# Attention and MLP on one core: two query groups share the first keys, half-size score operations at first, tiles turned by DMA, a larger tanh, W1 in halves

## The chip, the cores and the metric

One core of one Trainium2 chip. The metric is the device time of one execution in microseconds (us). Each run of a kernel was timed beside runs of the kernel before on the same chip. The span is the length of the profiled execution; the time is about 2 us more than the span in the same run.

Engines: PE does matrix products, PEld loads their weights, ACT does the exponentials and tanh, DVE and POOL do vector work, SP issues the DMA transfers. A q behind an engine's name in a view (SPq) is its sequencer, which issues.

## The reference

Input is x, 2048 rows of 1024. It is normalised by row, goes through attention of 32 heads of width 32 and, beside it, through a gated MLP of width 3584; all in bf16.

```python
xn = layernorm(x)
q, k, v = heads(xn @ wqkv)                      # 32 heads, width 32
p = softmax(q @ k.T * 32 ** -0.5)
s = heads_back(p @ v) @ wo
h = gelu_tanh(layernorm(xn) @ w1 + b1)
g = silu(h @ w2 + b2)
return x + s * g
```

## The kernel before

The kernel doesn't write instructions in the order in which they run. It makes operations with an assumed duration each; a list scheduler in the program, run once when the kernel is built, then fixes the order on every engine. I call its result the static order.

The assumed durations, and ACT's:

```python
def c_act(n):
    return 49 + 0.836 * n          # ns: 905 for 1024 elements
...
def chunk(item, fn, occ, R, mode="f", W=()):
    o = add("PE", lambda e, fn=fn, item=item: fn(e, item.bank), occ, TL, R, W, item=item, mode=mode)
```

The start. Tiles of 128 rows are normalised (statistics on DVE, the power and the normalising on POOL, the first two on DVE), turned on PE, and copied by ACT. Keys are projected by pairs of tiles:

```python
chunk(it, fn, n * 56, [("xnb", t % 4), ("ident",)])                 # turn a tile on PE
...
act(lambda e: e.activation(dst, src(), ACT.Copy), c_act(128 * n), [], W, 0, it)
...
pro_q += [tr_item(lo), tr_item(lo + 1), k_pair_item(n, False)]
```

A unit is four heads, 256 queries and one pair of key tiles: a score operation of eight matmuls and two exponentials of 128 x 1024. There are 512 units, so 1024 exponentials. Eight units make a group, whose sums over the keys stay in one bank of PSUM, where PE's results land, until it is normalised. Scores go round a ring of six banks; as long as the tiles come in (the first 8 units) four of them serve the scores and two more the projections and sums:

```python
NARROW = 8
k0 = 0 if u < NARROW else 2 * (u - NARROW) + 2
b0 = [(2 * k0 + j) % 6 for j in range(4)]
...
for h in range(2):
    x = act(lambda e, h=h: e.activation(P[pi][:, 2 * h:2 * h + 2].rearrange("p j k q -> p (j k q)"),
                                        ps[:, pr[h] * 1024:(pr[h] + 1) * 1024], ACT.Exp, scale=SCALE),
            c_act(1024), [("S", pr[h])], [("P", pi, h)], 0)
```

The tanh of the MLP is 512 wide. (The last four output items, of eight matmuls each, run after the last exponential.)

```python
act(lambda e: e.activation(ut_t[i3][:], ut_t[i3][:], ACT.Tanh, scale=GC * GA), c_act(512), ...)
```

The softmax here doesn't subtract the row's maximum and nothing guards it: scores larger than these inputs give would overflow.

## Time and profile before

| | before |
|---|---|
| time, median | 1061.66 us (1060.71 to 1061.72, 3 runs) |
| span of the profiled run | 1060.2 us, granted clock 0.998 |
| first exponential starts | 12.69 us |
| ACT's next work after the 32nd exponential starts (a tanh; before it the start, after it the full middle) | 63.45 us |
| last exponential ends | 1046.09 us |
| from there to the end of the span, "the tail" | 14.1 us |
| ACT busy / PE busy / DVE busy | 1028.9 / 1026.5 / 946.9 us |

Three views matter. The chain that ended last says which engine's work fills the span. The waits of an engine add up its idle time by what ended it. The timeline gives one row for a row of like operations: start, length, engine, line, operation, output and input, how many, and in brackets the idle time before and what ended it. I read the kernel as three parts: the start, the middle in which ACT is always busy, and the tail.

### The profile page before, as it was taken

The page shows a single profiled execution, that of the slowest core. Times are in us where ns is not written, and L with a number is a line of the kernel's source. Part 1 is how long each engine was busy: PE and PEld are TensorE (multiplying, and loading weights), DVE is VectorE, ACT ScalarE, POOL GpSimd, SP SyncE. Part 2 cuts the span into 40 slices and gives each one's busy share as a digit, 9 for nine tenths or more (in the row PEclk, how much of TensorE's full clock was granted, in tenths as well). Part 3 has the DMA queues.
Part 4 walks back from the last instruction along what each step waited for, and adds up shares of the span by engine and source line. Part 5 has one row for each costly group of instructions (what it writes and reads, how often), then busy time and mean ns, then how long its engine had stood idle before and what let it go on. Part 6 is the DMA issues. An engine that isn't in the chain of part 4 may idle for free.

```text
span 1060.2 us, 32647 instructions
## 1 busy us (share of the span) xinstructions
PE 1026.5 (97%) x14502; PEld 643.7 (61%) x14562; DVE 946.9 (89%) x1585; ACT 1028.9 (97%) x1186; POOL 31.2 (3%) x42
## 2 busy tenths in 40 slices
PE   7999999999999999999999999999999999999998
PEld 5756466556665566566665566466665666665443
DVE  8479898999999998899989998999999998978996
ACT  4999999999999999999999999999999999999994
POOL 5500000000000000000000000000000000000000
PEclk9999999999999999999999999999999999999999
DMA  9335166522674466423763476224765776662442
GB/s 268 111 96 158 42 179 190 144 76 71 186 207 126 113 193 196 113 57 112 206 192 105 122 199 195 74 76 121 212 180 151 221 217 190 179 197 70 134 140 87
DMA packets 285798, 156.52 MB, mean 148 GB/s; under 512 B 23642, under 2 KB 276570, under 8 KB 285658
## 3 DMA queue, kind: packets, MB, share of 16 engines
q1 hardware_dynamic: 285658, 154.44, 51.0%
q8 instruction: 114, 1.87, 0.8%
q14 instruction: 26, 0.21, 0.1%
HBM read 142.35 MB, written 12.06 MB: 146 GB/s over the span
## 4 chain that ended last, share of the span: by engine, by line
ACT 93%; PE 4%; DVE 2%; DMA 1%; issue 0%; SPq 0%; POOL 0%; POOLq 0%
ACT P L1067 86%; ACT ut L939 5%; PE ps L668 3%; ACT gw L971 2%; DVE stats L823 1%; DMA hT<-in_A_x_dram 1%; PE ps L663 1%; ACT big L814 0%; PE ps L1058 0%; PE ps L803 0%; DVE yT L911 0%; POOL gw L847 0%; DVE V L740 0%; DVE mv L825 0%; SPq L693 0%
## 5 line engine op out<-in xcount | busy, mean ns | idle before, releaser
L1067 ACT ACTIVATE P<-ps 128x1024 bf16<-128x1024 f32 x1024 | 986.8, 1243 | 5.3 <-PE ps L1058 5.3
L1087 DVE TENSOR_TENSOR PA<-P 128x2048 bf16<-128x2048 bf16 x243 | 294.7, 1215 | 25.4 <-ACT P L1067 24.1
L668 PE MATMUL ps<-yT,w1r 128*128 128x256 bf16 x1792 | 234.9, 275 | 2.3 <-DVE xb L931 1.1
L668 PE MATMUL ps<-w2r,hT 128*128 128x256 bf16 x1792 | 226.9, 273 | 0.3 <-DVE nv L1121 0.2
L668 PEld LDWEIGHTS ps<-yT,w1r 128*128 128x128 bf16 x1792 | 162.1, 98 | 60.5 <-issue 28.6
L668 PEld LDWEIGHTS ps<-w2r,hT 128*128 128x128 bf16 x1792 | 162.2, 98 | 51.0 <-issue 30.5
L1091 DVE TENSOR_TENSOR PA<-PA 128x1024 bf16<-128x1024 bf16 x219 | 147.7, 684 | 1.4
L663 PE MATMUL ps<-P,V 128*32 128x256 bf16 x4096 | 142.8, 274 | 0.6 <-DVE xb L931 0.4
L668 PE MATMUL ps<-big,qk 128*128 128x512 bf16 (+2 forms) x522 | 120.9, 357 | 5.7 <-issue 2.1
L668 PE MATMUL ps<-qk,big 128*128 128x256 bf16 (+1 forms) x723 | 121.2, 305 | 2.5 <-issue 1.3
L663 PEld LDWEIGHTS ps<-P,V 128*32 128x32 bf16 x4096 | 97.7, 96 | 33.1 <-issue 19.6
L1058 PE MATMUL ps<-QKT 32*128 32x256 bf16 x2048 | 101.7, 273 | 7.4 <-ACT P L1067 5.9
L1058 PE MATMUL ps<-qk 32*128 32x256 bf16 x2048 | 101.9, 273 | 6.2 <-ACT P L1067 2.1
L939 ACT ACTIVATE ut<-ut 128x512 f32<-128x512 f32 x112 | 94.5, 855 | 0.0
L668 PEld LDWEIGHTS ps<-qk,big 128*128 128x128 bf16 x736 | 65.3, 98 | 41.5 <-issue 13.3
L931 DVE TENSOR_TENSOR xb<-ps,b1T 128x512 bf16<-128x512 f32 x112 | 76.6, 684 | 13.9 <-PE ps L668 12.6
L941 DVE SCALAR_TENSOR_TENSOR hT<-ut,xb 128x512 bf16<-128x512 f32 x112 | 76.4, 684 | 5.9 <-ACT ut L939 5.2
L668 PEld LDWEIGHTS ps<-big,qk 128*128 128x128 bf16 x568 | 47.7, 98 | 52.4 <-issue 15.6
L1058 PEld LDWEIGHTS ps<-QKT 32*128 32x128 bf16 x2048 | 30.3, 92 | 76.6 <-ACT P L1067 75.9
L937 DVE SCALAR_TENSOR_TENSOR ut<-sq,xb 128x512 f32<-128x512 bf16 x112 | 76.1, 682 | 0.3
L1058 PEld LDWEIGHTS ps<-qk 32*128 32x128 bf16 x2048 | 30.4, 92 | 71.6 <-ACT P L1067 67.4
L663 PE MATMUL ps<-PA,ones 128*32 128x256 bf16 x1068 | 56.0, 274 | 0.3 <-DVE PA L1091 0.3
(75 smaller groups left out, 532.2 us busy)
## 6 DMA issues: line engine op xcount, KB each, us to landing
w1r<-in_B_w_dram SPq DMA_DIRECT2D x112, 512.0 KB, 4.4
w2r<-in_B_w_dram SPq DMA_DIRECT2D x128, 448.0 KB, 4.4
qk<-in_A_wqkv_dram SPq DMA_DIRECT2D x16, 256.0 KB, 3.2
g_scratch<-gw SPq DMA_DIRECT2D x32, 128.0 KB, 3.0
o_scratch<-ot SPq DMA_DIRECT2D x56, 64.0 KB, 2.8
big<-o_scratch SPq DMA_DIRECT2D x28, 128.0 KB, 3.5
hT<-in_A_x_dram SPq DMA_DIRECT2D x10, 256.0 KB, 5.5
qk<-in_A_wqkv_dram SPq DMA_DIRECT2D x4, 512.0 KB, 4.4
```

The source lines that it names most:

```text
L663: ins = e.matmul(dst(j), lhsT=lhsT(j), rhs=rhs(j), start=start, stop=stop, tile_position=(0, 32 * j), skip_group_check=True)
L668: return e.matmul(dst, lhsT=lhsT, rhs=rhs, start=start, stop=stop, skip_group_check=True)
L823: dve(lambda e, t=t, c=c: e.bn_stats(stats[:, t, c, :], xst[t][:, c * 512:(c + 1) * 512]), 600, [XS(t)], [("st", t, c)], 1)
L931: dve(lambda e: e.tensor_tensor(xb_t[i3][:].rearrange("p (k t) -> p k t", k=2), bank(it.bank).rearrange("p (k t) -> p k t", k=2), b1T[:, 2 ...
L937: dve(lambda e: e.scalar_tensor_tensor(ut_t[i3][:], sq_t[p % 2][:], 1.0 / GA, xb_t[i3][:], op0=ALU.add, op1=ALU.mult), c_f32(512), [("sq", ...
L939: act(lambda e: e.activation(ut_t[i3][:], ut_t[i3][:], ACT.Tanh, scale=GC * GA), c_act(512), [("ut", i3)], [("ut", i3)], 1)
L941: dve(lambda e: e.scalar_tensor_tensor(hT[:, hs].rearrange("p k t -> p (k t)"), ut_t[i3][:], 1.0, xb_t[i3][:], op0=ALU.add, op1=ALU.mult), ...
L971: act(lambda e: e.activation(zh_t[zi], z_t[zi], ACT.Tanh, scale=0.5), c_act(512), [("z", zi)], [("zh", zi)], 1)
L1058: ins = e.matmul(bank(b0[j], kk * 256, (kk + 1) * 256), lhsT=QKT[sl][32 * j:32 * j + 32, 1, kb * 128:(kb + 1) * 128], rhs=QKT[sl][32 * j:3 ...
L1067: x = act(lambda e, h=h: e.activation(P[pi][:, 2 * h:2 * h + 2].rearrange("p j k q -> p (j k q)"), ps[:, pr[h] * 1024:(pr[h] + 1) * 1024], ...
L1087: pa = dve(lambda e: e.tensor_tensor(PA_all[:, a0:a0 + 2].rearrange("p u j q -> p (u j) q"), P_all[:, p0:p0 + 2, :, 0, :].rearrange("p u j ...
L1091: pb = dve(lambda e: e.tensor_tensor(PA[a0][:], PA[a0][:], PA[a1][:], op=ALU.add), c_b16(1024), [("PA", a1)], [("PA", a0)], PBPRIO)
```

## The change

Its intent: take work off ACT, which carries the chain, and give it exponentials earlier.

1. From the third tile on, a tile is turned by a transposing DMA and not by PE and an ACT copy; tiles 2 and 3 are normalised on DVE.
2. The first two query groups share each pair of keys as it comes, so four exponentials come with each pair, not two.
3. For the first 16 units a score operation covers half a unit; both groups' sums are open in banks 4 and 5.
4. One tanh of 1024 takes the place of two of 512; the DVE operations around it are merged too.
5. The sums of P for the denominator are added over four units.
6. Seven of eight matmuls of the last four output items are summed and put aside early.
7. W1 comes in two halves, PE's pieces are single matmuls, and some constants differ.

The core of the diff, much cut:

```diff
-    NARROW = 8
-    plan.narrow = NARROW
+    NARROW = 16
+    plan.narrow = 2 * NARROW
...
         def c_act(n):
-            return 49 + 0.836 * n
+            return 52.5 + 0.836 * n
+
+        def c_acts(n):
+            return 92 + 0.836 * n
...
-            pro_q += [tr_item(lo), tr_item(lo + 1), k_pair_item(n, False)]
+            for t in (lo, lo + 1):
+                if t < TD:
+                    pro_q.append(tr_item(t))
+                else:
+                    add("SP", lambda e, t=t: e.dma_start_transpose(out=xnT[:, :, t * 128:(t + 1) * 128], in_=xnb[t % 4]),
+                        1290, 0, [("xnb", t % 4)], [("xnT", t, h) for h in range(2)], 0, sem=f"tp{t % 4}", nbytes=262144)
+            pro_q.append(k_pair_item(n, False))
...
-            act(lambda e: e.activation(ut_t[i3][:], ut_t[i3][:], ACT.Tanh, scale=GC * GA), c_act(512),
-                [("ut", i3)], [("ut", i3)], 1)
+            act(lambda e: e.activation(ut_t[i2][:], ut_t[i2][:], ACT.Tanh, scale=GC * GA), c_acts(1024),
+                [("ut", i2, 0), ("ut", i2, 1)], [("ut", i2, 0), ("ut", i2, 1)], 1)
...
-            plan.s_queue.append(o)
+            if u < NARROW:
+
+                for h in range(2):
+                    plan.s_queue.append(add("PE", lambda e, h=h: s_fn(e, (2 * h, 2 * h + 1)), 232.0, TL + 30, R, [("S", pr[h])], mode="r"))
+            else:
+                plan.s_queue.append(add("PE", lambda e: s_fn(e, range(4)), 235.0, TL + 30, R, [("S", pr[0]), ("S", pr[1])], mode="r"))
...
+                    for pos, (i, kp) in enumerate([(0, 0), (0, 1), (1, 0), (1, 1)] + [(i, kp) for kp in range(2, NKP) for i in range(2)]):
+                        x, vc = unit(i * 8 + kp, two[i], pos)
...
+                if qb == PART:
+
+                    for t2 in range(2):
+                        wo_load(NQB - 1, t2)
+                        for nh in range(2):
+                            wo_item(NQB - 1, t2, nh, 0, 7)
```

## The prediction

> **What bounds the kernel now.** I read the page first, then the waits of ACT, the groups of ACT and DVE by shape, and the timeline of the start and of the end. The page:
>
> ```profile
> span 1060.2 us, 32647 instructions
> ...
> PE 1026.5 (97%) x14502; PEld 643.7 (61%) x14562; DVE 946.9 (89%) x1585; ACT 1028.9 (97%) x1186; POOL 31.2 (3%) x42
> ...
> ACT 93%; PE 4%; DVE 2%; DMA 1%; issue 0%; SPq 0%; POOL 0%; POOLq 0%
> ```
>
> PE and ACT both read 97% busy, so the first row decides nothing; the chain that ended last does: 93% of it is ACT. The waits of ACT are three rows over the whole execution:
>
> ```profile
> ACT big L814 <- PE ps L803: 11.2, 7, 6.0
> ACT P L1067 <- PE ps L1058: 5.3, 5, 3.0
> ACT L715 <- PEq L1284: 0.7, 1, 0.7
> ```
>
> The 1024 exponentials waited only 5.3 us. The timeline of ACT shows where (start, length, what, idle before):
>
> ```profile
> 8.19 1.51 ACT L814 ACTIVATE big<-ps 128x1024 bf16<-128x1024 bf16 x2 [5.98 <-PE ps L803]
> 12.69 1.94 ACT L1067 ACTIVATE P<-ps 128x1024 bf16<-128x1024 f32 x2 [2.98 <-PE ps L1058]
> 16.01 1.02 ACT L814 ACTIVATE big<-ps 128x1024 bf16<-128x1024 bf16 x1 [1.38 <-PE ps L803]
> ...
> 22.49 1.95 ACT L1067 ACTIVATE P<-ps 128x1024 bf16<-128x1024 f32 x2
> ...
> 61.63 1.94 ACT L1067 ACTIVATE P<-ps 128x1024 bf16<-128x1024 f32 x2 [0.92 <-PE ps L1058]
> ```
>
> After 62 us ACT never waits again; the stretches 70 to 1043 us of the windows view are 100% ACT. So the span has three parts: a start in which ACT does copies and idles, a saturated middle, and a tail. In the chain, 29 exponentials in a row take 26.56 us, so one costs 0.9165 us of ACT, not the 1.243 us of its mean duration (neighbours overlap). Between 63.45 and 1045.73 us the exponentials and the small tanh fill all time; taking the exponentials out leaves 0.51 us for each 512-wide tanh.
>
> The account closes: first exponential 12.7; 1024 x 0.9165 = 938.5; 144 tanh x 0.51 = 73.4; 14 tile copies after the first exponential x 0.92 = 12.9; idle after the first exponential 1.38+0.15+2.46+0.63+0.21+0.19+0.35+0.50+0.68+0.92 = 7.5; tail from the last exponential's end at about 1045.7 to 1060.2, 14.5. The sum is 1059.5 of 1060.2. The tail is this:
>
> ```profile
> 1046.71 0.43 PEld L663 LDWEIGHTS ps<-P,ones 128*32 128x32 bf16 x16
> ...
> 1047.48 0.45 DVE L1118 STREAM_TRANSPOSE nt<-ps 128x256 f32<-128x256 f32 x1 [1.04 <-PE ps L663]
> ...
> 1049.15 0.41 DVE L1128 TENSOR_TENSOR qk<-ps,nt 128x256 bf16<-128x256 f32 x1
> ...
> 1056.86 0.69 DVE L1221 SCALAR_TENSOR_TENSOR w1r<-ps,w1r 128x512 bf16<-128x512 f32 x1 [0.58 <-PE ps L668]
> 1057.58 0.43 DVE L1228 TENSOR_TENSOR w1r<-w1r 128x512 bf16<-128x512 bf16 x1
> ```
>
> The normalised last group is ready at 1049.56, and the four output items of eight 512-wide matmuls then hold PE until 1056.8.
>
> **What the Trainium skill says.** "ScalarE: Activation LUTs", section What ACT_TABLE_LOAD costs: 0.833 ns per element plus 186 ns with immediates, back-to-back ones overlapping by about 93 ns. That is a fixed 93 ns per ACTIVATE; the trace agrees: 0.51 - 512 x 0.833/1000 = 0.083 us for the tanh and 0.063 us for the exponential. "VectorE: DVE Perf Modes", section The TRN2 errata, says that SBUF-source operations pay a fixed cost per instruction: the trace has 0.416 us for 512 and 0.684 us for 1024 bf16 elements of tensor_tensor, so 0.148 us fixed. "DMA: Bandwidth & Descriptors", section Latency and other measured facts, gives transposing DMAs 261 GB/s with a non-contiguous middle dimension, 350 to 400 otherwise. A tile of 262,144 bytes is then, as an estimate from that page, 0.7 to 1.0 us of transfer; no transposing DMA is in this trace. "TensorEngine Tiling (Array Packing)", Key Properties, says that a change of tiling mode drains TensorE: the trace shows about 0.2 us of idle weight load around each score operation.
>
> **The change part by part.**
>
> *Tile copies.* 14 of 16 tiles are turned by DMA. This takes 14 x 0.92 = 12.9 us off ACT and 14 x about 0.5 = 7 us off PE. They stood in the prologue, where they delayed exponentials, so I count them fully: -12.9 us, provided that exponentials are there to fill their place.
>
> *Two groups per key pair.* That provides them. Now each pair of key tiles releases one unit, 2 exponentials, 1.83 us; with two groups it releases 3.67 us. Supply per pair from the timeline: POOL needs 0.71+0.19+2x1.20 = 3.3 us; DVE 4 x 0.6 + 0.3 for statistics plus an evacuation, about 3.2 us. So 3.3 in against 3.67 out: once going, ACT should not starve. The gap after the first unit stays: ACT is done at about 14.5. Tiles 2 and 3 are now normalised on DVE (0.55 us each), which I place at 12.3 to 13.4; then a DMA issue, 2.5 to 3.5 us to land (plain loads of that size took 3 to 5.5 us, the longer ones in a queue), 0.9 us of projection, an evacuation of 0.4, the score: exponentials at 19 to 20. That is 4.5 to 5.5 us idle. I add 2 to 4 us for stalls in the half-unit stage: the two rings alternate with about 0.2 us semaphore, 0.2 chunk, 0.1 mode change, 0.25 score and 0.25 to ACT against 0.9165 us, which just doesn't fit every time. Idle 8 us instead of 7.5: +0.5 us.
>
> *Larger tanh.* 112 + 32 tanh of 512 become 56 + 16 of 1024: 72 fixed costs of 0.083 us: -6.0 us, directly on the path.
>
> *The tail.* Seven of eight matmuls of the last four output items are done earlier. After 1049.5 remain 4 x 0.22 us on PE, overlapped with 4 evacuations at 0.65, two f32 adds at 0.6 on DVE (two on POOL beside them), and 2.2 us for the store: the end about 5.5 us after the normalisation, against 10.6 now. The partial sums' own work lies under ACT. I take -4.5 us.
>
> *Sums over four units.* A third add on DVE, at most 123 x 0.684 = 84 us, and 28 more second adds (19 us) and 4 first ones (5 us), against 168 merged GELU operations and 16 gate products saving 0.148 us each (27 us): DVE would go from 947 to 1028 us, 99% of the new span. The schedule drops adds that come late, so I expect part of them. PE saves: 1276 ones-matmuls are 319 groups of four at 0.11 us, 35 us; at full use 160 remain, saving 17 us, with half the third adds dropped 11 us. PE isn't the bound, so 0 us, but it keeps PE behind ACT.
>
> *W1 in halves, smaller chunks, other issue constants.* Transfers already come in time; 0 us.
>
> The sum: -12.9 + 0.5 - 6.0 - 4.5 = -22.9 us; 1061.66 - 22.9 = 1038.8. A perfect start (the first gap only) would give about 1035.5. The schedule looks tuned against measured costs, so I lean to the better side: **1037.5 us**.
>
> **Rivals.** (a) *PE becomes the bound in the prologue.* From 19 to 46 us it must do six key projections (5.3), a query pair (0.9), two value items (3.5), 28 half scores at 0.23 plus two mode changes (11.8) and the first products (3.5): 25 of 27 us. Then five value items and twelve delayed products (14 us) meet ten units' scores (4.3) in 18.3 us. For it: PE is 30.1 of 33 us busy there now. Against: value items can wait. It would make 1040 to 1047.
> (b) *The transposing DMAs are slow or queue behind loads.* If a tile took over 1.83 us steadily, 12 tiles would lag: at 2.5 us, 8 us more, 1045 to 1047. Against: the loads beyond tile 7 and W1 are held back.
> (c) *DVE becomes the bound in the middle* and delays evacuations, then scores: merged operations of 1.2 us block it longer. For: 89% now, 96% or more after. Against: its own waits and the dropping of adds. It would make 1042 to 1060.
> (d) *PE in the middle.* Counting 0.11 us per 256-wide matmul, 0.22 per 512, 0.43 per score with changes gives some 1000 us now, 94%. ACT's gain squeezes it by 2%, the ones-matmuls return 1 to 1.7%: about neutral.
>
> **Range and chances.** Copies and tanh, 19 us, are nearly sure as work; what stalls give back is 0 to 10 us in the start and perhaps as much in the middle; the tail is 4 to 5. So 1028 to 1048 at 8 in 10. The line of 2% lies at 1040.4, three microseconds above my figure: faster 0.65, within 0.32, slower 0.03.
>
> **What would show it.** Right: ACT waits after the first exponential of 6 to 10 us, mostly one before 20 us; 32 exponentials done by about 48 us instead of 63; two ACT copies instead of sixteen; tanh of 1024 at 0.94 us; under 11 us after the last exponential; 100% ACT in the middle. Wrong: score waits spread over the middle (c, d), ACT waits of over 12 us before 60 us (a if PE is full there, b if PE waits for DMA), a first exponential later than 13.5 us, or transposes landing in over 4 us.

## The result, and the profile after

The changed kernel took 1057.97 us (median of 4 runs, 1056.18 to 1058.75); the kernel before took 1061.18 us (1060.6 to 1061.72) in the same rounds. Ratios here are the mean time of one kernel's fast runs over that of the other's of the same rounds, so not quite the ratio of the medians: 0.9967, 95% interval 0.995 to 0.9985. That is a real gain of 0.3% and within the 2% that count as the same. Predicted were 1037.5 us, with 1028 to 1048 as the range: 20 us too good. A gain of over 2% had been given 0.65, what came 0.32.

The page of the changed kernel, the rows that answer to those of before:

```profile
span 1055.8 us, 31978 instructions
...
PE 1024.0 (97%) x14230; PEld 632.8 (60%) x14230; DVE 967.9 (92%) x1463; ACT 1010.3 (96%) x1100; POOL 28.6 (3%) x40
...
ACT 88%; PE 7%; DMA 2%; DVE 2%; SPq 0%; POOL 0%; issue 0%; DVEq 0%; POOLq 0%
```

ACT lost 18.6 us of work, as predicted (12.9 of copies, some 6 of tanh), but the span lost only 4.4. ACT's share of the chain fell from 93% to 88%: PE and the DMA took its place. Its waits in the changed kernel (in all, times, longest):

```profile
ACT P L1134 <- PE ps L1120: 23.3, 8, 7.0
ACT big L845 <- PE ps L834: 7.2, 2, 6.4
```

Exponentials waited 23.3 us where it was 5.3. ACT's timeline in the changed kernel shows where:

```profile
15.25 1.94 ACT L1134 ACTIVATE P<-ps 128x1024 bf16<-128x1024 f32 x2 [4.21 <-PE ps L1120]
24.23 7.44 ACT L1134 ACTIVATE P<-ps 128x1024 bf16<-128x1024 f32 x8 [7.05 <-PE ps L1120]
...
44.00 1.94 ACT L1134 ACTIVATE P<-ps 128x1024 bf16<-128x1024 f32 x2 [1.59 <-PE ps L1120]
46.53 1.94 ACT L1134 ACTIVATE P<-ps 128x1024 bf16<-128x1024 f32 x2 [0.60 <-PE ps L1120]
50.68 7.51 ACT L1134 ACTIVATE P<-ps 128x1024 bf16<-128x1024 f32 x8 [2.21 <-PE ps L1120]
64.61 12.94 ACT L1134 ACTIVATE P<-ps 128x1024 bf16<-128x1024 f32 x14 [6.43 <-PE ps L1120]
```

All of it is in the start. The 32nd exponential ends at 58.19 us instead of 63.57, but the gap of 6.43 us behind it more than takes that back: ACT's next work, which was to come 12.4 us sooner, starts at 64.61 instead of 63.45 us. (Before, that is a tanh, and the 33rd exponential starts at 63.97; now it is the 33rd exponential.) From there on ACT is full, as before. The table by part:

| part | before | after | difference | predicted |
|---|---|---|---|---|
| start, to ACT's next work after 32 exponentials | 63.45 | 64.61 | +1.2 | -12.4 |
| middle, to the end of the last exponential | 982.6 | 977.0 | -5.6 | -6.0 |
| tail | 14.1 | 14.15 | 0 | -4.5 |
| span | 1060.2 | 1055.8 | -4.4 | -22.9 |

So 13.6 us are missing in the start, 4.5 in the tail, 0.4 in the middle. Four places show why.

**The second pair of keys.** PE's timeline of the changed kernel:

```profile
9.97 0.86 PE L834 MATMUL ps<-ident,gw 128*128 128x128 bf16 x8 [1.35 <-DVE gw L867]
10.62 3.38 PE L701 MATMUL ps<-big,qk 128*128 128x128 bf16 x32
...
19.04 1.05 PE L701 MATMUL ps<-qk,big 128*128 128x256 bf16 x8 [2.73 <-DMA big<-gw]
20.33 3.52 PE L701 MATMUL ps<-big,qk 128*128 128x256 bf16 x16 [0.23 <-DMA big<-yT]
23.78 0.42 PE L1120 MATMUL ps<-qk 32*128 32x256 bf16 x8
```

The 32 matmuls at 10.62 take 3.38 us; before they took 1.96. The granted clock between 10 and 14 us is 0.55 to 0.60 of full speed, after PE stood idle 0.98 and 1.35 us. The same comes back at 20.33: sixteen matmuls in 3.52 us after an idle stretch of 2.73, which ended when the transposed tile had come.

**The transposing DMA.** SP's issues in the changed kernel (start, time taken by the issue):

```profile
15.69 1.35 SPq L894 DMA_TRANSPOSE big<-gw  x1
17.09 1.29 SPq L894 DMA_TRANSPOSE big<-yT  x1
...
38.33 0.51 SPq L940 DMA_DIRECT2D w2r<-in_B_w_dram  x1
38.88 3.98 SPq L894 DMA_TRANSPOSE big<-gw  x2
42.90 0.58 SPq L933 DMA_DIRECT2D w1r<-in_B_w_dram  x1
43.52 1.24 SPq L894 DMA_TRANSPOSE big<-gw  x1
```

One issue takes 1.24 to 2 us of SP, in one row with the weight loads. Issued at 15.69, the tile is used at 19.04: 3.35 us. The DMA view of the first 60 us gives the median from issue to landing:

```profile
big<-gw SPq DMA_TRANSPOSE x10, 4.3
big<-yT SPq DMA_TRANSPOSE x4, 4.4
```

POOL normalises pairs at 19.29, 23.83, 27.99, 31.40, 35.78 and 39.40 us, one in about 4.0 us, not one in 3.3 as I had taken. The last pair's DMA is issued at 43.5 and 44.8 us, its keys are projected at 48.7.

**The change of ring.** From 48.7 us on no tile is missing, and yet ACT idles 6.43 us before 64.61. The windows view of the changed kernel (stretch, its length, busy PE, PEld, DVE, ACT, POOL, then clock, DMA share, GB/s):

```profile
48.70:63.70 15.00, 14.97 (x203) 9.60 (x199) 4.54 (x10) 7.51 (x8) 0.00 (x0) 1.00 0.84 203
```

PE is busy 14.97 of 15.00 us while ACT is busy half the time. The 17th unit is the first with whole score operations and needs banks 4 and 5. These hold the sums of the two groups that share keys, so all their products must be done first, and so all values of all tiles projected first. The chain over this stretch is PE throughout: value projections, products of P and V, the last two at 61.5; then DVE moves the sums out and makes the query tile, and the score starts at 64.17.

**The tail.** The end of PE's timeline in the changed kernel:

```profile
1042.46 1.69 PE L701 MATMUL ps<-qk,big 128*128 128x512 bf16 x7
1043.98 0.38 PE L701 MATMUL ps<-qk 128*128 128x512 bf16 x1
...
1045.92 1.67 PE L701 MATMUL ps<-qk,big 128*128 128x512 bf16 x7
1047.43 1.24 PE L701 MATMUL ps<-qk 128*128 128x512 bf16 x5
```

And of DVE's:

```profile
1043.92 0.42 DVE L1224 TENSOR_TENSOR qk<-ps,nt 128x256 bf16<-128x256 f32 x1
...
1048.46 2.48 DVE L1281 SCALAR_TENSOR_TENSOR w1r<-ps,w1r 128x512 bf16<-128x512 f32 x4
...
1051.70 1.28 DVE L1286 TENSOR_TENSOR w1r<-w1r,hT 128x512 bf16<-128x512 bf16 x2
```

The last group is normalised at 1044.34 us, but the four matmuls that wait for it come last on PE, at 1047.7, some 3.3 us later. Ahead of them PE does three whole output items of another group, 24 matmuls of 0.216 us, 5.2 us from 1042.5 on. Seven eighths of the last items had indeed been put aside; other work of PE had been put off into the tail in their place. What follows the four matmuls takes another 8.1 us, where the prediction had 5.5 for all that follows the normalisation: on DVE the other group's last evacuation and add (0.69 and 0.84 us in the chain) come in among the four evacuations (2.39), and the stores end 2.8 us after the last add.

### The profile page after: what moved, and what is told of

It is laid out like the page before. It is cut to its first block, busy times and chain, and to the rows that moved or that the text cites. A ratio compares the mean times of both kernels' runs of the same rounds, so it can differ in the third digit from the quotient of the medians.

```text
span 1055.8 us, 31978 instructions
## 1 busy us (share of the span) xinstructions
PE 1024.0 (97%) x14230; PEld 632.8 (60%) x14230; DVE 967.9 (92%) x1463; ACT 1010.3 (96%) x1100; POOL 28.6 (3%) x40
## 4 chain that ended last, share of the span: by engine, by line
ACT 88%; PE 7%; DMA 2%; DVE 2%; SPq 0%; POOL 0%; issue 0%; DVEq 0%; POOLq 0%
ACT P L1134 82%; ACT ut L995 5%; PE ps L701 5%; ACT gw L1031 1%; PE ps L696 1%; PE ps L1120 1%; DMA big<-yT 1%; DMA hT<-in_A_x_dram 1%; DVE ut L854 0%; DMA big<-gw 0%; DVE w1r L1281 0%; DVE V L771 0%; SPq L715 0%; POOL gw L886 0%; SPq L723 0%
## 5 line engine op out<-in xcount | busy, mean ns | idle before, releaser
L1134 ACT ACTIVATE P<-ps 128x1024 bf16<-128x1024 f32 x1024 | 965.3, 1245 | 23.4 <-PE ps L1120 23.3
L1164 DVE TENSOR_TENSOR PA<-P 128x2048 bf16<-128x2048 bf16 x246 | 298.7, 1216 | 15.8 <-ACT P L1134 15.1
L1169 DVE TENSOR_TENSOR PA<-PA 128x1024 bf16<-128x1024 bf16 x204 | 138.2, 681 | 1.5
L701 PE MATMUL ps<-big,qk 128*128 128x512 bf16 (+2 forms) x568 | 134.6, 368 | 1.5 <-DMA big<-gw 0.8
L701 PE MATMUL ps<-qk,big 128*128 128x256 bf16 (+1 forms) x736 | 127.3, 306 | 3.2 <-DMA big<-gw 2.7
L1120 PE MATMUL ps<-qk 32*128 32x256 bf16 x2048 | 106.0, 273 | 8.6 <-ACT P L1134 7.6
L701 PEld LDWEIGHTS ps<-qk,big 128*128 128x128 bf16 x736 | 64.9, 98 | 45.0 <-issue 17.7
L995 ACT ACTIVATE ut<-ut 128x1024 f32<-128x1024 f32 x56 | 72.5, 1295 | 0.0
L998 DVE SCALAR_TENSOR_TENSOR hT<-ut,xb 128x1024 bf16<-128x1024 f32 x56 | 67.9, 1212 | 1.3 <-ACT ut L995 1.0
L993 DVE SCALAR_TENSOR_TENSOR ut<-hT,xb 128x1024 f32<-128x1024 bf16 x56 | 68.0, 1214 | 0.0
L696 PE MATMUL ps<-PA,ones 128*32 128x256 bf16 x896 | 46.4, 275 | 0.0
```

Source lines behind the costliest of these rows:

```text
L696: ins = e.matmul(dst(j), lhsT=lhsT(j), rhs=rhs(j), start=start, stop=stop, tile_position=(0, 32 * j), skip_group_check=True)
L701: return e.matmul(dst, lhsT=lhsT, rhs=rhs, start=start, stop=stop, skip_group_check=True)
L993: dve(lambda e, r=r: e.scalar_tensor_tensor(ut_t[i2][:, r], h[:, r], 1.0 / GA, xb[:, r], op0=ALU.add, op1=ALU.mult), c_f32(r.stop - r.star ...
L995: act(lambda e: e.activation(ut_t[i2][:], ut_t[i2][:], ACT.Tanh, scale=GC * GA), c_acts(1024), [("ut", i2, 0), ("ut", i2, 1)], [("ut", i2, ...
L998: dve(lambda e, r=r: e.scalar_tensor_tensor(h[:, r], ut_t[i2][:, r], 1.0, xb[:, r], op0=ALU.add, op1=ALU.mult), c_f32(r.stop - r.start), [ ...
L1120: ins = e.matmul(bank(b0[j], kk * 256, (kk + 1) * 256), lhsT=QKT[sl][32 * j:32 * j + 32, 1, kb * 128:(kb + 1) * 128], rhs=QKT[sl][32 * j:3 ...
```

## The experiments

All kernels gave the right result, but for e5 to e7, which leave out products on purpose (the check doesn't notice them). Each was run five rounds (e5 to e7 three) beside the kernel before, four to six runs of each. What I read from each profile:

| kernel | time, median (range), us | ratio to before, 95% | first exp. | waits after it | last exp. ends | tail |
|---|---|---|---|---|---|---|
| before | 1061.18 (1060.6-1061.72) | | 12.69 | 2.3 | 1046.09 | 14.1 |
| after | 1057.97 (1056.18-1058.75) | 0.9967 (0.995-0.9985) | 15.25 | 19.1 | 1041.65 | 14.15 |
| e1 | 1065.03 (1062.92-1066.44) | 1.0036 (1.0023-1.0049) | 15.96 | 19.3 | 1049.28 | 14.1 |
| e2 | 1057.64 (1056.46-1058.94) | 0.9969 (0.9957-0.9982) | 15.04 | 11.6 | 1034.14 | 21.5 |
| e3 | 1060.67 (1060.37-1062.34) | 1.0003 (0.9991-1.0016) | 13.98 | 11.2 | 1044.93 | 13.8 |
| e4 | 1064.45 (1063.31-1066.46) | 1.003 (1.0017-1.0044) | 14.98 | 27.4 | 1050.25 | 14.15 |
| e5 | 1067.19 (1065.5-1067.75) | 1.0054 (1.0039-1.0069) | 12.36 | 7.0 | 1051.22 | 14.7 |
| e6 | 1064.73 (1062.71-1067.21) | 1.0041 (1.0022-1.006) | 14.82 | 23.8 | 1046.51 | 14.2 |
| e7 | 1054.57 (1053.69-1054.87) | 0.9936 (0.9921-0.9951) | 15.10 | 13.9 | 1037.51 | 14.1 |
| e8 | 1049.1 (1048.72-1050.11) | 0.9887 (0.9873-0.9902) | 13.99 | 11.2 | 1034.09 | 12.6 |
| e9 | 1065.11 (1063.23-1065.85) | 1.0035 (1.0022-1.0048) | 14.90 | 26.1 | 1049.54 | 14.2 |
| e10 | 1054.83 (1052.55-1055.71) | 0.9939 (0.9927-0.9951) | 14.95 | 12.8 | 1035.22 | 18.4 |
| e11 | 1057.04 (1054.85-1061.21) | 0.997 (0.9956-0.9984) | 14.74 | 8.0 | 1044.28 | 12.2 |
| e12 | 1052.27 (1050.6-1054.71) | 0.9924 (0.9912-0.9936) | 13.65 | 10.0 | 1036.10 | 12.2 |
| e13 | 1064.01 (1062.02-1067.61) | 1.0029 (1.0014-1.0043) | 12.55 | 2.0 | 1046.93 | 14.5 |
| e14 | 1062.13 (1060.57-1065.39) | 1.0012 (0.9999-1.0025) | 15.12 | 25.4 | 1049.66 | 12.6 |
| e15 | 1063.51 (1061.77-1064.04) | 1.0015 (1.0003-1.0027) | 14.81 | 23.0 | 1047.09 | 12.6 |
| e16 | 1058.44 (1054.7-1063.39) | 0.9977 (0.9958-0.9997) | 13.66 | 20.8 | 1041.65 | 14.15 |
| e17 | 1050.49 (1049.31-1052.16) | 0.9903 (0.9889-0.9917) | 13.45 | 13.9 | 1036.19 | 12.6 |
| e18 | 1049.56 (1048.23-1050.89) | 0.9888 (0.9872-0.9905) | 14.31 | 12.4 | 1035.61 | 12.6 |

The waits after the first exponential are those of exponentials for scores or products; copies' own waits are not in them. Where I subtract two experiments' times, their rounds may differ; the kernel before had medians of 1060.7 to 1061.7 in all of them. Parts 3, 5, 6 and 7 of the change were not undone by themselves; part 3 was extended (e2), and of part 6 only the order at the end was tried (e10, e15).

The theory at the outset: the change removes what the prediction said, but the start is not set by ACT any more. It is set by when keys come and by the change of ring, and the tail by what PE has left. The rival: the removed work itself was worth little, since PE bounds the whole kernel.

### One part undone: the tanh

```diff
-            act(... ut_t[i2][:] ..., ACT.Tanh ...), c_acts(1024), ...
+            for j in range(2):
+                act(... ut_t[i2][:, j * 512:(j + 1) * 512] ..., ACT.Tanh ...), c_acts(512), ...
```

(and the same for the gate's tanh)

> The changed kernel with each 1024-wide tanh of ACT issued again as two of 512; all else as changed. Theory 1 (ACT sets the pace from 65 us on, so its fixed costs count one for one): 72 more fixed costs of 0.078 to 0.083 us, 5.6 to 6.0 us slower than the changed kernel, 1063.5 to 1064 us. Rival (PE or DVE sets the pace in the middle and the merge was hidden): within 1 us of the changed kernel's 1058.0. ACT idle before 65 us as in the changed kernel, 19 us after the first exponential, in both.

The two-step tanh costs 7.1 us of time, against 72 x 0.083 = 6.0 worked out. The last exponential ends 7.6 us later, 1.2 of them waits of exponentials after 100 us. The merge is worth what the prediction said or a little more, so ACT does bound the middle; the time is 1 us above what theory 1 expected.

### The change of ring

```diff
+    NWIDE = 24
...
+            if n in (4, 5):
+                pro_q.append(q_pair_item(n - 2))
...
-            k0 = 0 if u < NARROW else 2 * (u - NARROW) + 2
+            k0 = 0 if u < NWIDE else 2 * (u - NWIDE) + 2
...
-            if u < NARROW:
+            if u < NWIDE:                     # half-unit scores for eight units more
```

> The changed kernel with half-unit scores on the two-pair ring up to unit 24 instead of 16, and the queries of group 2 projected while keys still come; sharing, DMA turning and sums as changed. Theory 1 (the 6.4 us wait before 64.6 us is the change of ring: the scores of unit 16 need PSUM banks 4 and 5, which hold both shared groups' sums until they are finished): that wait falls to under 1.5 us, 32 exponentials are done about 5 to 6 us earlier, and the time falls by 4 to 6 us to 1052 to 1054. Rival (PE's backlog is what counts; whatever ACT gains at the start comes back in the tail): the wait falls as well, but the tail after the last exponential grows from 14.6 to about 20 us and the time stays within 1.5 us of 1058.

The wait of 6.43 us is gone and the last exponential ends 7.5 us earlier, at 1034.14. The time is unchanged all the same, as the rival said. (The edit also projects the third group's queries early, which the first whole score reads. In the changed kernel five of the eight matmuls for them, 1.1 us, and their cast on DVE, 0.61 us, are in the chain before that score. So some 1.7 of the 6.43 us may be theirs and not the ring's; no run parts the two.) PE's timeline of this run, from its beginning of the tail to its end:

```profile
1034.76 0.61 PE L702 MATMUL ps<-qk,big 128*128 128x512 bf16 x2
...
1047.29 1.24 PE L702 MATMUL ps<-qk 128*128 128x512 bf16 x5
```

From the first of these on, 59 matmuls of output items come before the last four, where it was 24: (59 - 24) x 0.216 = 7.6 us. What ACT won at the start, PE gave back at the end. The gap is real, and filling it alone is worth nothing that the runs can tell.

### The tiles on PE again

```diff
-TD = 2
+TD = 16
```

> The changed kernel with all 16 tiles turned on PE and copied by ACT as before the change; sharing and the rest as changed. Theory 1 (the 12.9 us of copies taken off ACT turned into waiting for keys, since a turned tile takes over 3 us from DMA issue to use and the pairs come every 4.2 us): 14 copies come back, ACT's waiting after the first exponential falls from 19 us to 7 to 10 us, and the time stays within 4 us of 1058. Rival (the DMA turning pays its 12.9 us and the loss is elsewhere): 10 to 13 us slower, 1068 to 1071.

Fourteen copies, 12.9 us of ACT, came back and cost 2.7 us. The waits fell from 19.1 to 11.2: copies filled idle time. So in the kernel as changed, turning by DMA is worth 2.7 us, not 12.9, which was theory 1.

### One group after the other

```diff
-enumerate([(0, 0), (0, 1), (1, 0), (1, 1)] + [(i, kp) for kp in range(2, NKP) for i in range(2)])
+enumerate([(i, kp) for i in range(2) for kp in range(NKP)])
```

> The changed kernel with the 16 first units in the order group 0 then group 1, so that the groups do not share the keys as these come; all else as changed. Theory 1 (sharing fills waiting between the pairs, but only part of it): ACT waits 2 us or more at nearly every pair of keys, 20 to 25 us in all after the first exponential; the last of 32 exponentials is later by 1 to 5 us; time 1059 to 1063. Rival (sharing is itself what costs, as both groups' sums end together at the change of ring): faster than the changed kernel by 2 to 4 us, 1054 to 1056.

6.5 us slower, 1.5 us above theory 1's range, with 27.4 us of waits in place of 19.1. Sharing keys works, though with less effect than the DMA turning needs to pay.

### Less work for PE

```diff
-                    for f0 in range(0, 7, FINE):
+                    for f0 in range(0, 6, FINE):       # 256 of 1792 products left out: wrong on purpose
```

(in the kernel before: `for f0 in (0, 2, 4):`)

> The kernel before with 256 of the 1792 matmuls of the second MLP product left out (the result is wrong on purpose): 256 x 0.11 = 28 us less work for PE, nothing else removed. Theory 2 (before the change ACT set the end and PE had just enough time; PE's backlog at the last exponential was only some 10 matmuls, 2.2 us, beside the 32 that must come last): 0 to 3 us faster than before, 1058 to 1061. Rival (PE already set the end before the change): 8 us faster or more, under 1053.

> The changed kernel with the same 256 matmuls left out (wrong on purpose). Theory 2 (ACT's path still has its 19 us of waiting at the start and ends at about 1041; the 24 matmuls of earlier output items that stand before the last four in the tail are PE's backlog and go): the last exponential stays at 1040 to 1043 us, the tail shrinks from 14.6 to 9 to 11 us, time 1052 to 1055. Rival (the start's waiting is itself from a full PE): last exponential earlier by 5 us or more, under 1036.

> The kernel with half-unit scores up to unit 24, with the same 256 matmuls left out (wrong on purpose). In e2 the last exponential came 7.6 us earlier than in the changed kernel and the time did not move, as PE worked on for 15 us. Theory 2 (PE's total of work sets the end there, so the 7.6 us are to be had if PE has less): last exponential at 1032 to 1035, tail 9 to 12 us, time 1043 to 1048, 10 us or more faster than e2. Rival (the tail is a matter of order and of DVE and the stores, not of PE's amount): tail stays above 17 us, within 4 us of e2's 1057.6.

All three missed. Some 28 us of PE's work less (256 x 0.11) made the kernel before slower by 5.5 us and the changed one by 6.8, and the one of e2 faster by 3.1. ACT waits in the middle appear, 5.6 us in e5 and 4.7 in e6 between 100 and 1000 us, where the kernel before, the changed one, e2 and e3 have none, and the mean granted clock is 0.95 to 0.97 in 500 to 700 and 900 to 1030 us. The static order is another one and PE has pauses. The clock's record in the traces shows what lies between these and the waits: the mean of 0.97 is one short stretch at half clock. In e5 it lasts from 652.2 to 662.4 us. PE had stood idle for 1.94 us just before it (to 651.49), and ACT's longest wait, 2.40 us, ends in it, at 660.25. The windows view of e5, read as above:

```profile
642.00:652.20 10.20, 7.27 (x71) 3.13 (x69) 8.88 (x15) 10.20 (x14) 0.00 (x0) 1.00 0.42 117
652.20:662.40 10.20, 6.90 (x112) 3.35 (x112) 4.66 (x7) 7.70 (x10) 0.00 (x0) 0.50 0.01 2
```

The same shows in all twenty traces. Nine of them (e1, e4 to e7, e9, e11, e14 and e15) have such a stretch between 100 and 1000 us, each after pauses of PE of 0.5 to 2.3 us, and in these nine the exponentials wait 1.2 to 6.2 us in all there. The other eleven have none, and the exponentials wait 0.1 us at most. That the low clock makes the waits, and not the pauses by themselves, is not shown: no run filled these pauses. Why PE pauses there stays open too. The three runs do tell that "PE is short of time" is not a rule by which these kernels can be read: the order counts. In e7 the tail fell from 21.5 to 14.1, so the backlog is a matter of PE's work, as e2 said.

### Order re-timed, and the last items first

ACT's exponential takes 0.9165 us and the scheduler reckons 0.9086. The idea: it thinks ACT ahead of where it is, places each score too early, and PE stands waiting for the ring; what PE doesn't get done falls to the end.

```diff
-            return 52.5 + 0.836 * n
+            return 60.5 + 0.836 * n
...
-            return 92 + 0.836 * n
+            return 81 + 0.836 * n
...
-            a = dve(... [("nt", i)], 1, pv)
+            a = dve(... [("nt", i), ("nb", i)], 1, pv)           # a hidden order of two buffers made plain
...
-            plan.queues["wo"].append(it)
+            plan.queues["fin" if lo > 0 else "wo"].append(it)    # taken ahead of the others once ready
```

(with the edit of e2)

> Half-unit scores up to unit 24, the four last output items taken as soon as the last group is normalised instead of behind the items of the group before, the exponential and the 1024-wide tanh reckoned in the static order at what the trace shows (0.9165 and 0.937 us), one hidden write-after-read made explicit in the order; right results. Theory 2 (PE's work is unchanged, so the end moves only by what the order of the tail wastes: four evacuations, two adds and three stores one after the other after PE's last matmul, 7 us against 3.4 before): 2 to 5 us faster than e2, 1052 to 1056. Rival (ACT's 7.6 us can be had with a better order alone): 1046 to 1050.

1049.1 us, 12.6 below the kernel before in the same rounds and 8.9 below the changed one: the fastest of all, and in the range of the rival, not of theory 2. The last exponential ends where it did in e2, at 1034.09, and the tail is 12.6 instead of 21.5. The waits of PE's weight loads for the scores, between 100 and 1000 us, bear on why (in all, times, longest; "issue" is idle time for which the profile shows no cause); e2:

```profile
PEld ps L1123 <- ACT P L1137: 121.3, 441, 1.4
...
PEld ps L1123 <- issue: 1.7, 8, 0.2
```

and this run:

```profile
PEld ps L1123 <- ACT P L1137: 103.6, 380, 1.8
...
PEld ps L1123 <- issue: 13.2, 62, 0.3
```

The waits for exponentials fell by 17.7 us, but those without a cause on the same line rose by 11.5, so that PE waited 6.2 us less ahead of scores. It also had less to do: the other order drops fewer of DVE's additions, and 36 fewer matmuls with ones are left (908 instead of 944; four take 0.11 us, so 1.0 us in all). PE had 23 matmuls left for the tail besides the last four, where e2 had 59: 36 x 0.216 = 7.8 us, about what these two make. How much each is worth, no run shows.

### Which part of that made the gain

Each half of e8's edit by itself: the re-timing without half-unit scores (e9), half-unit scores and the last items first without the re-timing (e10), and re-timing with the last items first (e15). All three keep the line that makes the order of two buffers plain.

> The changed kernel with its static order worked out from the measured costs of ACT (0.9165 us per wide exponential, 0.937 us per wide tanh) and nothing else changed; this is one of the parts of the fastest run so far (1049.1 us, which also has half-unit scores up to unit 24, a query projection moved early and the last four output items taken at once). Theory 1, the parts need each other: the waits of ACT after the first exponential stay at 17 to 21 us, because the change of ring at unit 16 and the slow arrival of tiles are untouched; the time is 1055 to 1059 us. Rival, the re-timing is the gain by itself, since PE then waits less for exponentials and has nothing left for the tail: the weight-load waits for P fall by about 20 us as in the fastest run, the tail is under 13.5 us, the time 1049 to 1053 us.

> The fastest run so far without its re-timing: half-unit scores up to unit 24, the query projection early, the last four output items taken as soon as the group is normalised. Theory 1: the backlog of PE at the end is matmuls that the static order deferred because it reckons ACT faster than it is; taking the last four items first changes only who comes last, so the tail stays at 18 to 22 us and the time at 1054 to 1058 us. Rival, the order of the last items alone made the gain: a tail of 13 to 15 us, the time 1048 to 1051 us.

> The changed kernel re-timed, with the last four output items taken at once, but with the change of ring at unit 16 as it was: the fastest run without its half-unit scores up to unit 24 and the early query projection. Theory 1: the gap of 6.4 us at the change of ring stays and is passed on to the end, so the last exponential ends at 1040 us or later, the tail is 12 to 13.5 us, the time 1053 to 1058 us. Rival, the waits in the middle and at 106 us that the re-timed kernel showed come back too: 1060 to 1065 us. Third, the gap is made up elsewhere: 1048 to 1051 us.

Re-timing alone is a loss: 1065.11, 7 us over the changed kernel. The gap at the ring is still there (6.55 us), new waits stand at 106 us (3.38, for a product of P and V) and between 953 and 974 us (2.8 in three). Theory 1 got the start right and the time wrong. With the last items first (e15) it is 1063.51: the tail falls from 14.2 to 12.6 and the time by 1.6. The intervals of e9 and e15 overlap, so the 1.6 us are shown by the traces' tails and not by the times; the expected 1053 to 1058 was missed and the rival of e15, that the middle waits return, was right. Half-unit scores with the last items first (e10) give 1054.83; its tail is 18.4. I had the tail right and the time at the low end.

So the parts need each other: from e2, the last items first bring 2.8 us, and the re-timing on top of these 5.7. Why re-timing without half-unit scores brings the waits in the middle stays open: there the static order differs everywhere, and I took no part of it away by itself. The link is that of e5 and e6: e9's clock is at half from 102.4 to 105.8, 948.9 to 955.8 and 969.4 to 972.8 us, after pauses of PE, and each of its four waits ends in such a stretch or within 1.2 us of it.

As a control, the kernel before with its own assumed costs corrected (60.5 and 81 ns fixed in place of 49):

```diff
-            return 49 + 0.836 * n
+            return (60.5 if n > 512 else 81) + 0.836 * n
```

> The kernel before with its static order worked out from the measured costs of ACT (wide exponential 0.9165 us, 512-wide tanh 0.51 us), nothing else changed. A control: is the 11.6 us of the fastest run a gain of the change's parts, or would the kernel before have had it from re-timing? Theory 1: ACT of the kernel before is full from 62 us on and its tail has no backlog, so there is nothing to win: 1058 to 1064 us. Rival, re-timing by itself is the gain: under 1054 us.

1064.01 us, 0.3% slower. The gain of e8 is not had by re-timing the kernel before: it needs the change, with its start and its end mended.

### The parts of the change, in e8

```diff
-TD = 2
+TD = 16        # e11; e12: TD = 6
```

and, for e14, the edit of e4.

> The fastest run so far (1049.1 us) with all sixteen tiles turned on PE and copied by ACT, so 14 copies of 0.92 us are back. In the changed kernel the same edit cost only 2.7 us of 12.9, which I explained by ACT standing idle in the start anyway. Theory 1: here ACT idles after its first exponential only about 11 us, of which one gap of 6.35 us at the first pairs would be filled by copies; the edit costs 5 to 9 us: 1054 to 1058 us. Rival, the copies are hidden again and the DMA turning is worth little in any setting: 1049 to 1052 us.

> The fastest run so far with tiles 2 to 5 also turned on PE and copied by ACT, so that only tiles 6 to 15 wait for a transposing DMA. Theory 1: the first gap (6.35 us before the second pair's scores) is the latency of the first two transposing DMAs, 3.2 us each plus their issue; four copies cost 3.7 us of ACT but mostly in that gap, and the waits of ACT after the first exponential fall to 6 to 8 us: 1045 to 1048 us. Rival, the pairs of keys come no earlier since normalisation on POOL and DVE sets their pace: the copies are added, 1050 to 1053 us.

> The fastest run (1049.1 us) with the two groups one after the other instead of sharing the keys as they come. In the changed kernel this edit cost 6.5 us. Theory 1: the waits of ACT after the first exponential rise from 11 us to 18 to 22 us and all of it comes out at the end: 1055 to 1060 us. Rival, the end is set by PE whatever ACT does in the start: 1049 to 1052 us.

With the ring's gap gone, turning tiles by DMA is worth 7.9 us (e11) instead of 2.7, and sharing keys 13.0 (e14) instead of 6.5. e14's expectation missed on the large side by 2 us. So these parts are worth more when nothing else sets the pace, though turning tiles still less than the 12.9 us that the prediction said. (3.8 us of new waits at 97 to 103 us, about a stretch at half clock, are in e11's 7.9.) In e12, where tiles 2 to 5 are turned on PE again, the first gap falls from 6.35 to 2.78 us, which shows that it was the wait for the DMA; but four copies and a gap of 4.07 us (1.89 in e8) before the last pair's exponentials at 48.43 us take it back: 1052.27, slower. That gap too is a wait for the DMA: the last tile's is issued at 40.56 us and PE waits for it until 45.41, 4.85 us. Both its theories missed in part; the rival, with 1050 to 1053, had the time.

### The clock in the start

Dummy matmuls (512 wide, results thrown away) in the stretches where PE stood idle; the rest of the order stays the same. e16 is the changed kernel, e17 is e8, with four dummies after the turning of tile 0; e18 is e17 with ten more before the second pair's keys.

```diff
-                pro_q += [tr_item(0), qk_tile_item(0), ...
+                pro_q += [tr_item(0), fill_item(("xnb", 0), 4), qk_tile_item(0), ...
...
+            if n == 1:
+                pro_q.append(fill_item(("xnb", 2), 10))              # e18 only
```

> The changed kernel with four dummy matmuls (512 wide) between the turning of tile 0 and that of tile 1, where PE stood idle 1.35 us; the results are thrown away and the rest of the order is the same. Theory 1: PE's idle stretches are what lowered the clock to 0.55 to 0.60 between 10 and 14 us; with them filled the first projection of 32 matmuls takes 1.95 us instead of 3.38, the first exponential starts at 13.6 to 14.1 us instead of 15.25, and the time falls by about 1.2 us, to 1056 to 1057.5 us. Rival, the clock in the start differs from execution to execution whatever PE does: the first exponential stays at 14.8 us or later in the profile, the time within 0.5 us of 1058.

> The fastest run with the same four dummy matmuls. Its profile showed the clock at full speed from 4.7 us on and the first exponential at 13.99 us although PE idled as long as in the changed kernel; its timed runs were 2.4 us above that profile. Theory 1: the timed runs often had the low clock, and the dummies take that away: 1047 to 1048.5 us. Rival, no change: 1048.7 to 1049.7 us.

> The previous kernel (fastest run and four dummy matmuls) with ten more dummies ahead of the key projection of the second pair of tiles, where PE stood idle 3.5 us for the transposing DMA and then ran at 0.57 of its clock until 24 us: 8 matmuls in 1.89 us, 16 in 3.23. Theory 1: what the first dummies won was lost to that; with both stretches filled the 24 matmuls take 2.9 us instead of 5.1, the second exponentials start at 21.8 to 23 us instead of 24.29, the keys of the later pairs come no sooner than before since their DMA sets them, and the time falls by 0.5 to 2 us: 1048.5 to 1050 us. Rival, the low clock comes whatever PE does: the second exponentials stay at 24 us or later, the time at 1050 to 1051 us.

e16's profile did just what theory 1 said of the first exponential: it starts at 13.66 us, not 15.25. (One profile can't show that the dummies did it: e8's has a full clock there without them.) PE's timeline of e16:

```profile
10.58 1.95 PE L701 MATMUL ps<-big,qk 128*128 128x128 bf16 x32
...
18.33 1.89 PE L701 MATMUL ps<-qk,big 128*128 128x256 bf16 x8 [3.50 <-DMA big<-gw]
20.01 3.62 PE L701 MATMUL ps<-big,qk 128*128 128x256 bf16 x16
```

And the time didn't move: 1058.44, with a wide range of 1054.7 to 1063.39, which goes with the mean clock of the execution (0.999 in the fastest, 0.993 in the slowest). The second exponentials start at 24.21 us against 24.23, the later ones at 46.53, 50.68 and 64.61 in both kernels, the last one ends at 1041.65 in both. The 1.6 us were lost in the next gap, which grew from 7.05 to 8.61: PE now idled 3.50 us for the DMA, and the low clock came then (8 matmuls took 1.89 us against 1.05 in the changed kernel). So the late first exponential, which the account of waits counts as 2.6 us, cost nothing. e17 says the same: first exponential at 13.45, time 1050.49, a little over e8; both expectations for it were too low.

With both stretches filled, PE's timeline of e18:

```profile
19.83 1.05 PE L702 MATMUL ps<-qk,big 128*128 128x256 bf16 x8 [2.05 <-DMA big<-gw]
21.56 1.92 PE L702 MATMUL ps<-big,qk 128*128 128x256 bf16 x16 [0.69 <-DMA big<-yT]
```

The clock is 1.00 throughout and the 24 matmuls take 2.97 us instead of 5.1, as expected. But the tiles came later in this run: issued at 14.86 and 16.26 us, used at 19.83 and 21.56, 5.0 and 5.3 us. The second exponentials start at 23.85, not at 21.8 to 23. The time, 1049.56, is in the range of theory 1, but its interval (0.9872 to 0.9905) overlaps e17's and e8's: nothing is shown of a gain. What the three show together: with dummies in both stretches the clock stays full (a mean of 0.998 to 0.999 in all four executions of e18, 0.995 to 0.998 in e17's), and the second pair then waits for the DMA alone.

## Why the prediction was wrong, step by step

**Tile copies, -12.9 us: the step that failed.** The copies went (two are left) and the figure of their cost was right. The prediction counted them "fully: -12.9 us, provided that exponentials are there to fill their place", and took that condition as met by the next step. It wasn't: e3 gives 2.7 us, the start as a whole +1.2 instead of -12.4.

**Two groups per key pair, "3.3 in against 3.67 out".** The supply was worked out from POOL and DVE alone. With turning by DMA, SP's issues (1.24 to 2 us each, in line with weight loads) and 4.3 us to landing are in the row, and DVE waits in its fixed order for key projections. Measured: one pair in about 4.0 us; in the trace before they were already 3.6 us apart on POOL, not 3.3. The tile of the second pair was to land in 2.5 to 3.5 us and took 3.35 from issue to use, or 5.0 to 5.3 in e18; the exponentials placed at "19 to 20" came at 24.23, since normalising (15.1 instead of 12.3) and the clock (3.52 us for what takes 1.92) added up before it.

**The half-unit stage's stalls, 2 to 4 us.** Those between 24 and 51 us were 5.7. But the change of ring behind it, 6.43 us, was not in the sum at all. The rival (a) had the mechanism: "five value items and twelve delayed products", PE full. It was set aside with "value items can wait". In the code they can't: banks 4 and 5 hold both groups' sums until every value is projected, and the first whole score needs these banks. e2 shows it, but for the 1.7 us named there: with half-unit scores for eight more units the values do wait and the gap goes.

**The tail, -4.5 us.** Two terms failed. The prediction gave PE no other work there: of the 24 matmuls of other items, some 3.3 us lie between the normalisation and the last four. And what follows these was put too short: 8.1 us, and 8.3 in e8, where the prediction had 5.5 from the normalisation on. e9 to e15, the same kernel but for the order of the last items, puts 1.6 us on that; e8's tail of 12.6 is the best but for e11 and e12 (12.2), and 9.6 was predicted. (The prediction read the tail before as 14.5 us; from the last exponential's end it is 14.1.)

**Larger tanh, -6.0 us.** Right: -5.6 between the two traces, 7.1 in e1. The 0.083 us counted for each is the trace's figure; the 93 ns with which the prediction says that the trace agrees are somewhat more than that and than the exponential's 63 ns.

**The middle neutral.** Right: ACT is at 100% from 64.61 on. The rivals (c) and (d), DVE or PE as the bound there, did not come; DVE is 967.9 us busy, far under the 1028 feared. The sums over four units left 264 groups of four ones-matmuls (896 + 160 single ones), not 160, so 59 of the 123 third adds and 43 of the 247 second ones were dropped, as guessed.

**Rivals (a) and (b)** were each given too little: both came, and with them the tail. The signs named for them, ACT waits of over 12 us before 60 us and transposes landing in over 4 us, are both in the trace, as is a first exponential later than 13.5 us. The last turned out to be harmless (e16). Of the signs for being right, 32 exponentials were done at 58.2 us and not at about 48, and 14.15 us followed the last one, not under 11.

What of the 13.6 us missing in the start belongs to what: 7.5 to the change of ring and the queries behind it (e2, by the end of the last exponential). The other 6 lie in how keys come; e16 to e18 exclude the clock at the first exponential, e12 shows that the DMA's delay sets the first gap. No run has made the pairs come in 3.3 us, so that this alone is the rest is argued, not shown.

Behind both is one thing: ACT was the bound only while the rest kept up with little to spare. PE, at 97% in both kernels, had 32 to 34 us of idle time in the span. It was the next bound at the change of ring and in the tail; at the second pair of keys that was the DMA, with the clock.

## What to carry to other kernels

Before counting work that is taken off the bound engine, ask at each place what would come next when it is gone: a saving in the start counts only if the next inputs are there, and a saving at the end only if the next engine has nothing left over. Ask where a scarce buffer changes hands (here two PSUM banks between two stages): the wait is there, whatever the sums of busy time say. Where a static order is built on assumed durations, correct these together with the change and time the whole, since one edit without the other can lose (e9) and both can win (e8). And read the clock's record beside the waits: in these traces the waits in the middle stand where pauses of PE were followed by half clock.

## What the Trainium skill lacked or had wrong

- "DMA: Bandwidth & Descriptors", section Latency and other measured facts, gives the transposing DMA's bandwidth but no time from issue to use, which here paced the second pair of keys. For a tile of 128 x 1024 bf16 from SBUF to SBUF the runs show 3.35 us from issue to use (the changed kernel's first, issued behind one load of x), 4.3 to 4.4 us to landing in the median among other loads, 5.0 to 5.3 from issue to use in e18, and 1.24 to 2 us of SP per issue.
- "TensorE: Matmul & The Clock Gate", section Part 1: The HAM clock gate, says that the clock drops to half after an idle window of some 3.4 us, which is free-running. Of shorter pauses it tells as well, in another kernel, but gives no length. Here idle stretches of 0.98 and 1.35 us with work between them were followed by half clock from 10.2 to 13.6 us in the changed kernel, and one of 1.94 us by 10.2 us of it in the middle of e5, while in e8 stretches of 1.80 and 1.32 us at the same place left it at 1.00. So idle stretches well under 3.4 us can be enough, and whether they are differs between traces, which agrees with a free-running window. With dummies of 0.9 us, which cut the second stretch to 0.55 and 0.48, the clock was 1.00 there (e16, e17).
- No page says that less work for PE can slow a kernel that ACT bounds: with 256 matmuls fewer, e5 and e6 took 5.5 and 6.8 us longer, with 3.4 to 13.7 us at half clock at a time in the middle and ACT's waits there. Whether the clock or the pauses before it make the waits is open.
